# Row maxima and the scores' second product in bfloat16, a ScalarE copy of the products with v, and a new plan of times

## Chip, core and metric

The kernel runs on one core of one Trainium2 chip, as one launch. The metric is device time in microseconds (us), the median of three runs. Engines are named as in the profile: PE is TensorE (matmuls; PEld its weight loads), DVE is VectorE, ACT is ScalarE, POOL is GpSimd, SP is SyncE, which here only issues DMAs.

## What is computed

Attention over queries that are averaged in pairs, then four experts that are mixed per token, then a gated block. Only the attention is touched by the change.

```python
# q, k, v: (2, 8, 1152, 64) float32: 16 heads; q and k drawn wide (about 0.62 standard deviation)
q_pool = q.reshape(B, H, S // 2, 2, D).mean(axis=3)          # 576 queries for each head
scores = scale * np.matmul(q_pool, k.transpose(0, 1, 3, 2))  # 576 x 1152
scores = scores - np.max(scores, axis=-1, keepdims=True)
attn = np.exp(scores)
attn = attn / (np.sum(attn, axis=-1, keepdims=True) + 1e-09)
x = np.matmul(attn, v)
...
x = _moe_ref(x=x, **moe_kwargs)      # 1152 tokens, 512 wide, 4 experts of 1024
return _moe2_ref(x=x, **moe2_kwargs)
```

## The kernel before

The 16 heads go in 8 pairs (`i` = 0 to 7); `s` = 0 or 1 is the head within a pair. For each head there are 9 blocks of 128 keys (`c`), 5 blocks of queries (`j`) and these steps.

- **Transposes.** PE turns the keys (`kt`, line 275) and the pooled queries (`qt`, 329) into PSUM. Both are then split into a float32r high part (`KAB`, `QH`, by ACT, lines 278 and 341) and a rest (`KL`, `QL`, by DVE, 281 and 332). `QZ` holds the queries of both heads, each with zeros in the other head's partitions (ACT lines 342 and 338, POOL 336). The transposes share three PSUM banks (`ps_w`) with the maxima.
- **Spread.** SP copies the parts into `K1` (high, twice), `Q1` (high over rest), `K2` (rest) and `Q2` (high) by DMA (`plan_spread`, 352).
- **Row maxima.** `mp` (line 390): for each query block, three products of `QZ` with 384 columns of `KAB`; DVE reduces the first two in one instruction and the third in another (393). The maxima are joined (407 to 410), turned by PE (`mr`, 425), split (`mh` by ACT, `ml` by DVE) and placed in the first two rows of `Q2` by four small DMAs, so that the score product subtracts them. They are made for pair `i + 1` while pair `i` has its scores.
- **Scores.** `s` (544): for each key block four products of 288 columns, two with `K1`, then two with `K2`, in one of two PSUM slots (`ps_s`). ACT takes the exponential (`pf`, 554), POOL what bfloat16 left of it (`pl`, 565).
- **Products with v.** `av` (587 and 589): 135 matmuls of 64 or 65 columns for each head, half a pair behind the scores, into one PSUM bank (`ps_a`). `vt` holds v scaled, high part by ACT (519) and rest by DVE (523); `vs` is its scale (454 to 458). At the end `out_of` divides by the sums: three DVE instructions (593, 597, 599), for the second batch a fourth (604). The bank is then free for the next head.

**What sets the order.** Each step is put on one list with a time by `at(t, f)`; the list is sorted by time and recorded. Each engine then runs its instructions in that order and waits on semaphores. A unit of time is an 18th of a pair. The constants at the file's top (`KH`, `LO`, `AVW`, `SPOS`, `MX0`, ...) are these times; they change an order, not a speed.

```python
        t = 18 * i
        plan_scores(i, 0, t)
        plan_scores(i, 1, t + 9)
        plan_av(i, 0, t + 9 + AV0, AVN)
        plan_av(i, 1, t + 18 + AV0, AVN if nx else 2)
...
    for _, _, f, args in sorted(agenda, key=lambda x: x[:2]):
        f(*args)
```

A tile name in a profile or an order is the tile's name with its numbers left out (`s`, `mp`, `av`); with numbers, `s3_0_1` is pair 3, head 0, key block 1, and a last number counts tiles.

Of the kernel before, what the change touches and what calls it, by code (L numbers as in the profile page):

```python
# [27 lines left out]
AV0 = 1.49
AVN = 7.48
AVW = ((0.64, 0.05, 1.06, 0.45, 1.0, 0.14, 0.2, 2.36), (0.8, 1.47, 1.71, 2.49, 0.72, 0.32, 0.55, 1.54))  # L30
VH = 0.8
VL = 2.36
VL0 = -5.71
VR = 4.82
VE = 0.2
# [29 lines left out]
KT = (3.05, 3.5)  # L65
QT = 4.54
MX0 = (7.0, 8.1, 9.35, 12.27, 13.06)
SPOS = ((0, 0.8, 2.1, 3, 4.4, 5, 6.2, 7, 7.9), (0.1, 1, 2.1, 3, 4, 5, 6, 7, 7.65))
# [1283 lines left out]
```

## Time and profile before

| | |
|---|---|
| median of three runs | 812.59 us (812.47 to 813.15) |
| the profiled execution | 812.85 us, of which the span from first to last instruction is 811.1 us |
| PE busy | 794.8 us, 98% of the span |
| DVE, ACT, POOL busy | 593.3, 396.0, 295.7 us |
| attention | about 19 to 252 us of the span |
| experts and gated block | the rest; from 300 us on neither code nor plan differs |

One execution was recorded. Matmuls overlap: one lasts longer in the trace than the time after which the next starts, so a price of PE work is read here from the start of one group to the start of the next. A row's time is from the span's start.

### The profile page before, as it was taken

The numbers are of one execution on the slowest core, as the hardware profiler recorded it, in microseconds if no ns is written. First come the engines' busy times: TensorE is split into PE (matmuls) and PEld (weight loads), VectorE is DVE, ScalarE is ACT, GpSimd is POOL, SyncE is SP. The second block draws the span as 40 slices with busy tenths as digits, with TensorE's granted clock in tenths as the row PEclk, the third lists the DMA queues.
The fourth block names the chain that finished last, engine by engine and source line by source line (L and its number), as shares of the span: only waits on it lengthen the run. The fifth ranks groups of instructions, "written<-read, shape, count | busy, mean of one in ns | idle before, by whom it ended". The sixth has DMA issues, their size and how long they took to land.

```text
span 811.1 us, 15625 instructions
## 1 busy us (share of the span) xinstructions
PE 794.8 (98%) x6301; PEld 522.8 (64%) x6301; DVE 593.3 (73%) x1065; ACT 396.0 (49%) x722; POOL 295.7 (36%) x277
## 2 busy tenths in 40 slices
PE   8799999999999999999999999999999999999998
PEld 6598889888877555555545555555554446655787
DVE  6878877887875666779878999979888877872000
ACT  2555565565484443434435556546554544553111
POOL 5787888798750000001101125203331223442100
PEclk9999999999999999999999999999999999999999
DMA  7967776783720121223313332221466842200011
GB/s 184 218 156 163 185 155 135 170 204 83 170 60 2 53 105 53 78 78 104 105 52 104 104 105 83 100 78 52 108 144 127 168 141 74 85 1 1 15 52 52
DMA packets 85975, 83.27 MB, mean 103 GB/s; under 512 B 49624, under 2 KB 67408, under 8 KB 85904
## 3 DMA queue, kind: packets, MB, share of 16 engines
q1 hardware_dynamic: 85904, 82.29, 39.3%
q8 instruction: 49, 0.80, 0.4%
q14 instruction: 22, 0.18, 0.1%
HBM read 51.92 MB, written 2.36 MB: 67 GB/s over the span
## 4 chain that ended last, share of the span: by engine, by line
PE 86%; DVE 10%; DMA 1%; ACT 1%; issue 1%; SPq 0%; ACTq 0%
PE dn L758 21%; PE up L718 21%; PE gt L1290 12%; PE s L544 8%; PE o L1306 6%; PE wf L1259 5%; PE av L589 5%; PE mp L390 5%; DVE mx L393 3%; PE av L587 2%; DVE vt L523 1%; PE kt L275 1%; DVE vs L457 1%; DVE ql L332 1%; DMA rk<-in_k 1%; DMA rw<-in_moe_w 1%
## 5 line engine op out<-in xcount | busy, mean ns | idle before, releaser
L758 PE MATMUL dn<-w,h 128*128 128x512 f16 x840 | 183.9, 379 | 0.0
L565 POOL TENSOR_TENSOR pl<-pf 128x576 f16<-128x576 f32 x141 | 162.7, 1175 | 48.7 <-ACT pf L554 47.5
L718 PEld LDWEIGHTS <-w 128*128 128x128 f16 x1152 | 111.5, 98 | 76.3 <-DVE w L689 0.8
L758 PEld LDWEIGHTS <-h 128*128 128x128 f16 x840 | 81.4, 98 | 96.5 <-ACT up L724 0.7
L554 ACT ACTIVATE pf<-s 128x576 f32<-128x576 f32 x144 | 92.4, 650 | 64.3 <-PE s L544 63.1
L393 DVE TENSOR_REDUCE mx<-mp 128x1 f32<-128x768 f32 (+1 forms) x144 | 101.9, 751 | 19.3 <-PE mp L390 18.7
L718 PE MATMUL up<-xB,w 128*128 128x320 f16 x768 | 109.9, 299 | 0.5 <-DVE xB L807 0.5
L544 PE MATMUL s<-Q,K 128*128 128x288 f32 x576 | 109.2, 313 | 0.2
L857 POOL TENSOR_TENSOR wo<-wo,cv_a 128x512 f32<-128x512 f32 x20 | 25.8, 1293 | 224.7 <-DVE wo L854 127.1
L724 ACT ACTIVATE up<-up 128x320 f32<-128x320 f32 (+1 forms) x96 | 45.8, 477 | 114.3 <-PE up L718 94.1
L718 PE MATMUL up<-xA,w 128*128 128x512 f16 x384 | 89.1, 379 | 0.3 <-DVE w L689 0.3
L589 PE MATMUL av<-vt,pf 128*128 128x65 f16 x720 | 85.0, 194 | 0.1
L544 PEld LDWEIGHTS s<-Q,K 128*128 128x128 f32 x576 | 82.0, 189 | 2.4 <-issue 0.6
L587 PE MATMUL av<-vt,pf 128*128 128x64 f16 x720 | 83.0, 194 | 0.0
L589 PE MATMUL av<-vt,pl 128*128 128x65 f16 x720 | 82.8, 195 | 0.0
L729 DVE TENSOR_TENSOR h<-up,h 128x320 f16<-128x320 f32 (+1 forms) x94 | 50.2, 551 | 42.7 <-ACT h L725 42.3
L1290 PEld LDWEIGHTS <-mw 128*128 128x128 f16 x576 | 55.9, 98 | 36.9
L589 PEld LDWEIGHTS <-pf 128*128 128x128 bf16 x720 | 66.9, 99 | 7.0 <-issue 1.3
L587 PEld LDWEIGHTS <-pf 128*128 128x128 bf16 x720 | 67.0, 98 | 6.9 <-issue 3.3
L589 PEld LDWEIGHTS <-pl 128*128 128x128 f16 x720 | 67.2, 98 | 3.4 <-issue 1.1
L390 PE MATMUL mp<-kab,QZ 128*128 128x384 f32 x216 | 56.5, 367 | 4.4 <-DVE mx L393 2.1
L772 DVE SCALAR_TENSOR_TENSOR x2B<-dn,sh,x2B 128x512 f32<-128x512 f32 x75 | 52.9, 744 | 4.7 <-PE dn L758 4.0
(184 smaller groups left out, 1171.3 us busy)
## 6 DMA issues: line engine op xcount, KB each, us to landing
rw<-in_moe_w SPq DMA_DIRECT2D x64, 512.0 KB
K<-kab SPq DMA_DIRECT2D x32, 288.0 KB
rk<-in_k SPq DMA_DIRECT2D x16, 288.0 KB
rv<-in_v SPq DMA_DIRECT2D x8, 576.0 KB
Q<-qh SPq DMA_DIRECT2D x32, 144.0 KB
K<-kl SPq DMA_DIRECT2D x16, 288.0 KB
rq<-in_q SPq DMA_DIRECT2D x8, 512.0 KB
rw<-in_moe_w_out SPq DMA_DIRECT2D x8, 512.0 KB
```

Source lines behind the costliest of these rows:

```text
L390: mm(ps[:, n, :PC], QZ[:, o : o + P], KAB[i][:, sl], start=True, stop=True)
L393: nc.vector.tensor_reduce(out=mx[i, s][:, j, g : g + 1], in_=st.pop((j, g))[:, :, :PC], axis=AX.XY, op=ALU.max)
L544: mm(ps[:, n, :HALF], a[s][:, cs], b[s][:, n * HALF : (n + 1) * HALF], start=first, stop=not first,)
L554: nc.scalar.activation(out=two(pft[i, s][:, c, :]), in_=st["s"][:, :, :HALF], func=AF.Exp, scale=SCORE)
L565: nc.gpsimd.tensor_tensor(out=o, in0=f, in1=h, op=ALU.subtract)
L587: mm(t[:, j, 0:D], p, vt[s][:, c, 0:D], start=False, stop=False)
L589: mm(t[:, j, :], p, vt[s][:, c, D:], start=(c == 0 and n == 0), stop=(c == NC - 1 and n == 2))
L718: mm(p, w[:, a, c, fc * P : (fc + 1) * P], x[b][:, c, lo - o : hi - o], start=(c == 0 and a == b), stop=(c == KD - 1 and a == 1),)
L729: nc.vector.tensor_tensor(out=hl[:, fc, lo:hi], in0=st["p"], in1=hh[:, fc, lo:hi], op=ALU.subtract)
L758: mm(p, hid[n][a][:, fc, t * P : (t + 1) * P], w[:, b, fc, :], start=(fc == 0 and a == b), stop=(fc == 1 and a == 1),)
L772: nc.vector.scalar_tensor_tensor(out=acc, in0=st["p"], scalar=share, in1=acc, op0=ALU.mult, op1=ALU.add)
L1290: mm(p, mws[n][:, a, m * KD + c], x[:, b * KD + c, lo - o : hi - o], start=(c == 0 and a == b), stop=(c == KD - 1 and a == 1),)
```

## The change

- `K2`, `Q2`, `QZ`, `KL` and the two parts of the maxima (`mh`, `ml`) become bfloat16; `K1`, `Q1`, `KAB`, `QH`, `QL` stay float32r.
- A bfloat16 copy `KB` of the transposed keys is added (`short`, on ACT, one of three on DVE for pair 0); the maxima are taken of `QZ` with `KB`.
- The bfloat16 product comes first in each score group.
- `Q2` is filled from `QZ` by two DMAs instead of from `QH` by one.
- `leave` copies the finished products with v from PSUM into an SBUF tile `as` on ACT. It is put on the list at `t + span + OUT`, `out_of` at `t + span + OUT + OUT2` with `OUT2 = -0.1`.
- The table of times is new.

```diff
-LO = 2.45
+LO = 4.1
...
-    K2 = [k_p.tile([P, S], F32R, name=f"K2_{s}") for s in range(2)]
+    K2 = [k_p.tile([P, S], BF16, name=f"K2_{s}") for s in range(2)]
...
-    Q2 = [k_p.tile([P, T], F32R, name=f"Q2_{s}") for s in range(2)]
...
-    QZ = k_p.tile([P, 2 * T], F32R, name="QZ")
+    Q2 = [k_p.tile([P, T], BF16, name=f"Q2_{s}") for s in range(2)]
...
+    QZ = k_p.tile([P, 2 * T], BF16, name="QZ")
...
+            KB[i] = kq_p.tile([P, S], BF16, tag="kb", bufs=1, name=f"kb{i}")
+            KL[i] = ha_p.tile([P, S], BF16, tag=f"ha{i % 2}", name=f"kl{i}")
...
+            def short(g=g, rows=rows):
+                nc.scalar.copy(out=rows(KB[i]), in_=st[g][:, :, :PC])
...
+            at(t + KT[g] + KH + KS, short)
...
+        def low_k():
+            nc.sync.dma_start(out=K2[s][64:128], in_=KL[i][r])
+
+        def short_q():
+            o = T + TL if s else 0
+            nc.sync.dma_start(out=Q2[s][64:128, : NB * P], in_=QZ[r, o : o + NB * P])
+            o = T if s else NB * P
+            nc.sync.dma_start(out=Q2[s][64:128, NB * P :], in_=QZ[r, o : o + TL])
...
-                mm(ps[:, n, :PC], QZ[:, o : o + P], KAB[i][:, sl], start=True, stop=True)
+                mm(ps[:, n, :PC], QZ[:, o : o + P], KB[i][:, sl], start=True, stop=True)
...
-                nc.vector.tensor_copy(MT[:, 0, :].bitcast(F32R), mf)
+                mb = tiny.tile([P, NB + 1], BF16, tag="mb", bufs=1, name="mb")
+                nc.vector.tensor_copy(mb, mf)
+                nc.vector.tensor_copy(MT[:, 0, :], mb)
...
-                for a, b, first in ((K1, Q1, True), (K2, Q2, False)):
+                for a, b, first in ((K2, Q2, True), (K1, Q1, False)):
...
+        def leave():
+            if (i, s) < (NPAIR - 1, 1):
+                x = tiny.tile([P, NB + 1, D + 1], F32, tag="as", name=f"as{i}_{s}")
+                nc.scalar.copy(out=x, in_=st["t"])
+                st["t"] = x
...
-        at(t + span + OUT, out_of)
+        at(t + span + OUT, leave)
+        at(t + span + OUT + (OUT2 if (i, s) < (NPAIR - 1, 1) else 0), out_of)
```

Three places show how the rows move. The first is PE at the start of pair 3, from the last product with v of head (2, 0); line 544 of before is line 572 of after, 390 is 416. Before:

```order
L589 MATMUL av2_0_1734<-vt0_119,pl2_0_1408 128x65
L544 MATMUL s3_0_0_1973<-Q1_0_125,K1_0_121 128x288 x2
L544 MATMUL s3_0_0_1973<-Q2_0_127,K2_0_123 128x288 x2
L544 MATMUL s3_0_1_1990<-Q1_0_125,K1_0_121 128x288 x2
L544 MATMUL s3_0_1_1990<-Q2_0_127,K2_0_123 128x288 x2
L390 MATMUL mp3_1_3_0_1996<-kab3_1486,QZ_129 128x384 x2
L390 MATMUL mp3_1_3_1_1999<-kab3_1486,QZ_129 128x384
```

The same place after:

```order
L617 MATMUL av2_0_1762<-vt0_119,pl2_0_1429 128x65
L572 LDWEIGHTS K2_0_123
L572 MATMUL s3_0_0_2003<-Q2_0_127,K2_0_123 128x288
L572 LDWEIGHTS K2_0_123
L572 MATMUL s3_0_0_2003<-Q2_0_127,K2_0_123 128x288
L572 MATMUL s3_0_0_2003<-Q1_0_125,K1_0_121 128x288 x2
L416 LDWEIGHTS QZ_129
L416 MATMUL mp3_1_3_0_2024<-kb3_1496,QZ_129 128x384
L416 LDWEIGHTS QZ_129
L416 MATMUL mp3_1_3_0_2024<-kb3_1496,QZ_129 128x384
L416 LDWEIGHTS QZ_129
L416 MATMUL mp3_1_3_1_2027<-kb3_1496,QZ_129 128x384
```

The last maximum product of the pair stands behind one score group instead of two; a bfloat16 product has a weight load of its own in the list, a float32r one carries it within. The second place is ACT at the same point of the program: `vt0` is the high part of v (519, now 547), `pf3_0` are the exponentials, `kab4` and `kb4` the keys of the next pair. Before:

```order
L554 ACTIVATE pf3_0_1971<-s3_0_0_1973 128x576
L519 ACTIVATE vt0_119<-rv3_1206,vs3_1597 128x9x64
L554 ACTIVATE pf3_0_1971<-s3_0_1_1990 128x576
L554 ACTIVATE pf3_0_1971<-s3_0_2_2017 128x576
L429 CAST mh3_1_2061<-mr3_1_2048 5x128
L278 CAST kab4_2050<-kt4_0_2052 128x768
L554 ACTIVATE pf3_0_1971<-s3_0_3_2042 128x576
L278 CAST kab4_2050<-kt4_1_2074 128x384
L554 ACTIVATE pf3_0_1971<-s3_0_4_2109 128x576
```

After:

```order
L547 ACTIVATE vt0_119<-rv3_1316,vs3_1629 128x9x64
L622 COPY as2_0_2022<-av2_0_1762 128x325
L582 ACTIVATE pf3_0_2001<-s3_0_0_2003 128x576
L582 ACTIVATE pf3_0_2001<-s3_0_1_2032 128x576
L582 ACTIVATE pf3_0_2001<-s3_0_2_2048 128x576
L457 CAST mh3_1_2080<-mr3_1_2066 5x128
L282 CAST kab4_2068<-kt4_0_2071 128x768
L285 CAST kb4_2069<-kt4_0_2071 128x768
L582 ACTIVATE pf3_0_2001<-s3_0_3_2060 128x576
L282 CAST kab4_2068<-kt4_1_2102 128x384
L285 CAST kb4_2069<-kt4_1_2102 128x384
L582 ACTIVATE pf3_0_2001<-s3_0_4_2111 128x576
```

`vt0` and the new copy `as2_0` now stand ahead of the pair's first exponential, and each cast of keys is followed by a second one. The third place is DVE where the products of head (2, 0) are divided, after the change:

```order
L419 TENSOR_REDUCE mx3_1_1839<-mp3_1_2_1_1944 128x1
L627 TENSOR_SCALAR dn2_0_2016<-av2_0_1762,vs2_1056 128x5
L631 RECIPROCAL dn2_0_2016<-dn2_0_2016 128x5
L633 TENSOR_TENSOR x0_117<-av2_0_1762,dn2_0_2016 128x5x64
L419 TENSOR_REDUCE mx3_1_1839<-mp3_1_3_0_2024 128x1
```

The division still reads `av2_0`, the PSUM tile, as before, since `out_of` is recorded ahead of `leave`; no row of any engine has an `as` tile as an input. This holds for all 15 copies.

## Rows read from the trace of the kernel before

**Rows 1.** Windows: stretch, its length, busy us by engine, PE clock, DMA share, GB/s.

```profile
19.00:50.00 31.00, 26.44 (x261) 21.55 (x261) 25.13 (x45) 15.62 (x28) 22.87 (x22) 1.00 0.83 190
50.00:77.50 27.50, 27.29 (x390) 24.34 (x387) 22.24 (x39) 16.03 (x27) 23.23 (x23) 1.00 0.71 164
105.10:132.70 27.60, 27.32 (x392) 24.38 (x389) 22.43 (x39) 16.05 (x27) 23.27 (x23) 1.00 0.74 163
187.90:215.50 27.60, 27.43 (x393) 24.42 (x390) 22.56 (x41) 16.05 (x27) 22.35 (x22) 1.00 0.59 137
215.50:252.00 36.50, 34.95 (x545) 28.82 (x542) 24.83 (x50) 21.92 (x38) 18.26 (x16) 1.00 0.30 71
300.00:811.00 511.00, 506.72 (x2751) 285.74 (x2749) 365.03 (x660) 233.65 (x442) 105.78 (x88) 1.00 0.29 82
```

**Rows 2.** Timeline of PE, pair 3 and before it: start, us, instruction, wait before it.

```profile
102.18 0.76 PE L544 MATMUL s<-Q,K 128*128 128x288 f32 x4
102.78 0.20 PE L589 MATMUL av<-vt,pl 128*128 128x65 f16 x1
...
103.22 0.80 PE L390 MATMUL mp<-kab,QZ 128*128 128x384 f32 x3
103.86 0.20 PE L587 MATMUL av<-vt,pf 128*128 128x64 f16 x1
...
105.12 1.29 PE L544 MATMUL s<-Q,K 128*128 128x288 f32 x8
106.25 0.68 PE L390 MATMUL mp<-kab,QZ 128*128 128x384 f32 x3
...
108.94 0.82 PE L275 MATMUL kt<-ident,rk 128*128 128x128 f32 x6
...
116.04 0.80 PE L390 MATMUL mp<-kab,QZ 128*128 128x384 f32 x3 [0.17 <-DVE ql L332]
...
119.09 0.79 PE L544 MATMUL s<-Q,K 128*128 128x288 f32 x4
119.71 0.68 PE L390 MATMUL mp<-kab,QZ 128*128 128x384 f32 x3
120.23 0.69 PE L544 MATMUL s<-Q,K 128*128 128x288 f32 x4
120.76 0.20 PE L589 MATMUL av<-vt,pf 128*128 128x65 f16 x1
...
132.74 1.30 PE L544 MATMUL s<-Q,K 128*128 128x288 f32 x8
```

**Rows 3.** Timeline of PE among the experts' products, 16-bit operands.

```profile
306.26 2.75 PE L718 MATMUL up<-xA,w 128*128 128x512 f16 x12
308.85 3.42 PE L718 MATMUL up<-xB,w 128*128 128x320 f16 x24
...
312.11 2.11 PE L718 MATMUL up<-xA,w 128*128 128x512 f16 x9
```

**Rows 4.** Groups by line, 0 to 420 us: count | busy, mean ns | idle before.

```profile
L725 ACT CAST h<-up 128x320 f16<-128x320 f32 x32 | 13.6, 426 | 1.0
...
L278 ACT CAST kab<-kt 128x768 fp32r<-128x768 f32 x7 | 5.6, 797 | 2.6 <-DMA Q<-qh 1.8 <-PE kt L275 0.9
```

**Rows 5.** Timeline of ACT within pair 3.

```profile
113.13 0.63 ACT L342 CAST QZ<-qt 64x576 fp32r<-64x576 f32 x1
...
119.29 0.78 ACT L519 ACTIVATE vt<-rv,vs 128x576 f16<-128x576 f32 x1 [0.93 <-PE av L589]
119.98 0.65 ACT L554 ACTIVATE pf<-s 128x576 f32<-128x576 f32 x1
```

**Rows 6.** Timeline of DVE within pair 3.

```profile
116.70 1.42 DVE L393 TENSOR_REDUCE mx<-mp 128x1 f32<-128x768 f32 x2 [0.71 <-PE mp L390]
...
120.19 0.49 DVE L599 TENSOR_TENSOR x<-av,dn 128x320 f32<-128x320 f32 x1
```

**Rows 7.** Line 457: durations of one in ns, min/median/max, first and last start.

```profile
L457 DVE TENSOR_SCALAR vs<-vs x8: 169/1045/1102, 19.2 to 196.8; 128x2 f32<-128x2 f32 x8
```

More of the change, by code (lines that the diff above doesn't have):

```diff
@@ L11 @@
 TURN = 1.03
-TURNS = (1.08, 1.18, 2.08, 2.53)
+TURNS = (1.18, 1.53, 1.63, 3.03)
 TURN0 = (0.05, 0.45, 0.55, 0.65)
-KH = 0.49
-KL_ = 0.62
-QH_ = 1.1
+KH = 0.39
+KL_ = 0.27
+QH_ = 1.2
 QL_ = 0.25
-M0 = 0.4
+M0 = 0.25
 M1 = 0.01
@@ L22 @@
 LASTD = ((4,), (0, 7))
-LOL = 0.85
+LOL = 0.95
+KS = 0.1
+KS0 = 0.01
 EX = 0.79
 EX2 = 0.85
-LO = 2.45
+LO = 4.1
 LOV = 1.15
[L28 to L35, printed above, removed]
+AV0 = 1.54
+AVN = 7.33
+AVW = ((0.4, 0.05, 0.51, 0.58, 1.25, 0.14, 0.4, 2.95), (0.48, 0.19, 1.03, 2.49, 1.4, 0.51, 0.69, 1.54))
+VH = 0.65
+VL = 1.91
+VL0 = -2.26
+VR = 4.02
+VE = 1.85
 V1 = (5.5, 1.4)
@@ L38 @@
 QZ0 = 0.25
-QZ1 = 0.1
-VLZ = 2.55
+QZ1 = 0.0
+VLZ = 2.2
 K0 = 1.2
@@ L44 @@
 LV2 = 15.6
-PQ = 0.52
-PQS = 0.65
+PQ = 2.17
+PQS = -0.75
 SH = -5.85
@@ L64 @@
 LATER = 0
[L65 to L68, printed above, removed]
+KT = (3.05, 4.05)
+QT = 4.99
+MX0 = (7.0, 8.15, 9.5, 11.52, 13.11)
+SPOS = ((0, 1.1, 1.95, 2.8, 4.3, 4.9, 6.5, 7, 7.5), (0.1, 0.6, 1.7, 2.7, 4.1, 4.4, 5.55, 7.0, 7.95))
 AVS = 0.02
-AVP = 2.35
+AVP = 1.7
 MXF = (7.3, 8.3, 10, 11.72, 13.01)
-MX1 = (14.0, 16.2, 17.25, 18.82)
-ME = 0.12
+MX1 = (14.15, 16.15, 17.2, 18.67)
+ME = 0.17
 SW = 130.8
 W1 = 133.8
-WT = ((123.5, 129.6, 130.6, 132.7, 138.5, 133.3, 133.5, 135.6, 135.8), (2, 8.8))
+WT =  ((124.7, 129.6, 130.6, 132.7, 138.5, 133.3, 133.5, 135.6, 135.8), (4.4, 8.95))
 WN = (1, 4, 5, 3, 0)
@@ L85 @@
 DT = (140.8, 144.1)
-OUT = 0.35
+OUT = 0.8
+OUT2 = -0.1
 XB = 148.6
@@ L204, in tile_kernel @@
     rq, rt, rk, rv = {}, {}, {}, {}
-    KAB, KL, QH, QL = {}, {}, {}, {}
+    KAB, KL, KB, QH, QL = {}, {}, {}, {}, {}
     pft, pht, plt = {}, {}, {}
@@ L301, in pe, with short @@
                 nc.tensor.transpose(st[n][:, m * P : (m + 1) * P], rk[0][:, 3 * n + m], ident)
+        def short(n):
+            dst = KB[0][:, n * PC : (n + 1) * PC]
+            if n == 1:
+                nc.vector.tensor_copy(dst, st[n])
+            else:
+                nc.scalar.copy(out=dst, in_=st[n])
         def hi(n):
@@ L317, in plan_k_now @@
             at(t + 0.1 * n, pe, n)
+            at(t + 0.1 * n + KS0, short, n)
             at(t + 0.1 * n + 0.05, hi, n)
@@ L362, in plan_spread @@
             cp(Q1[s][64:128], lambda: QL)
-            cp(K2[s][64:128], lambda: KL)
-        cp(Q2[s][64:128], lambda: QH)
+            at(t, low_k)
+        at(t, short_q)
     mx = {}
@@ L427, in cut_hi @@
         def cut_hi():
-            m = st["h"] = tiny.tile([NB + 1, P], F32R, tag="mh", bufs=1, name=f"mh{i}_{s}")
+            m = st["h"] = tiny.tile([NB + 1, P], BF16, tag="mh", bufs=1, name=f"mh{i}_{s}")
             nc.scalar.copy(out=m, in_=st["r"][: NB + 1, 0, :P])
         def cut_lo():
-            m = st["l"] = tiny.tile([NB + 1, P], F32, tag="ml", bufs=1, name=f"ml{i}_{s}")
-            nc.vector.tensor_tensor(out=m, in0=st["r"][: NB + 1, 0, :P], in1=f32(st["h"]), op=ALU.subtract)
+            m = st["l"] = tiny.tile([NB + 1, P], BF16, tag="ml", bufs=1, name=f"ml{i}_{s}")
+            nc.vector.tensor_tensor(out=m, in0=st["r"][: NB + 1, 0, :P], in1=st["h"], op=ALU.subtract)
         def place():
-            for n, m in enumerate((f32(st["h"]), st["l"])):
-                dst = f32(Q2[s][n : n + 1])
+            for n, m in enumerate((st["h"], st["l"])):
+                dst = Q2[s][n : n + 1]
                 nc.sync.dma_start(out=dst[:, : NB * P], in_=m[:NB])
@@ L866, in tile_kernel @@
         for s in range(2):
-            nc.gpsimd.memset(f32(Q2[s][0:64]), 0.0)
-            nc.gpsimd.memset(f32(K2[s][0:64]), 0.0)
-            nc.gpsimd.memset(f32(K2[s][0:3]), -1.0)
-            nc.gpsimd.memset(f32(Q2[s][0:3]), -SHIFT)
+            nc.gpsimd.memset(Q2[s][0:64], 0.0)
+            nc.gpsimd.memset(K2[s][0:64], 0.0)
+            nc.gpsimd.memset(K2[s][0:3], -1.0)
+            nc.gpsimd.memset(Q2[s][0:3], -SHIFT)
             nc.gpsimd.memset(vt[s][:, :, 128:129], 1.0)
@@ L873, in tile_kernel @@
         nc.vector.memset(QP[TL:P, NB], 0.0)
[L874 to L875 removed]
+        nc.vector.memset(QZ[64:128, :T], 0.0)
+        nc.vector.memset(QZ[0:64, T:], 0.0)
         nc.vector.memset(ones, 1.0)
```

8 lines of the change are left out of this document (3 added, 5 removed).

## The prediction

> **What bounds the kernel now.** I read the windows by stage first, then PE's timeline of one pair, then what PE waits for there.
>
> Of the 811.1 us, 511 stand behind 300 us with PE busy 506.7 [rows 1]: nothing there is touched. The attention has three parts. The first pair (19 to 50) takes 31.0 us with PE busy 26.4: its first half is a chain of maxima, not PE work. Six pairs follow, 27.6 us each (105.12 to 132.74 in [rows 2]; the first and the last of the six windows look like the middle one) with PE busy 27.3, POOL 23.3, DVE 22.4, ACT 16.0 [rows 1]. The last pair (215.5 to 252) has no maxima left and PE busy 34.95 of 36.5. So PE sets the pace from 50 to 252 us; behind it POOL has 4.3 us to spare in a pair, DVE 5.2, ACT 11.5. A saving on PE of more than that meets the next engine.
>
> **The change, part by part.**
>
> *Score groups.* Four float32r products behind a product with v take 102.78 - 102.18 = 0.60 us [rows 2]. Two groups in a row take 106.25 - 105.12 = 1.13, so the second costs 0.53: 0.132 for each product, and about 0.08 for entering float32r from 16-bit work, whose loads are too short to cover a float32r load. For 16-bit products: 12 of 512 columns in 308.85 - 306.26 = 2.59 us, 0.216 each; 24 of 320 in 312.11 - 308.85 = 3.26, 0.136 each [rows 3]; that is 0.00042 us a column, so 288 columns cost 0.1225 and 384 cost 0.1625 (estimates from these rows). A new group enters with a bfloat16 product, which needs no long load, and costs 2 x 0.1225 + 2 x 0.132 = 0.51. I take this since a float32r load is already hidden behind a product of 288 columns in the 0.53 group; if the entry price merely moves to the third product it is 0.59. Of 18 groups in a pair some 16 cost 0.60 now: 16 x 0.09 + 2 x 0.02 = 1.5 us saved in a pair (0.2 if the entry price stays).
>
> The Trainium skill (TensorE: Matmul & The Clock Gate, section LDWEIGHTS) puts a load at its columns over 1.2 in ns, 107 for 128. By that the load for `K1` fits under the second bfloat16 product, the group is 0.51, and the 0.59 falls away. No row here has a float32r load behind a 16-bit product of 288 columns, so I keep both ends.
>
> *Maxima.* Three products take 0.52 to 0.53 behind scores (119.71 to 120.23), 0.64 behind products with v (103.22 to 103.86) [rows 2], and 3 x 0.1625 = 0.49 in bfloat16. With six groups of the first kind and three of the second that is 6 x 0.04 + 3 x 0.15 = 0.7 us in a pair. PE's work falls by some 2.2 us.
>
> *ScalarE.* Two casts for `KB` repeat those of `KAB`: 0.80 [rows 4] and, for half the columns, about 0.48. Two copies of 325 columns out of PSUM cost about 0.43 each (the 320-column cast of [rows 4], 0.426). That is 2.1 us more in a pair, 18.2 in all, which fits. But ACT takes things in order. The order shows the copy right behind `vt` and ahead of the first exponential. In the trace `vt` starts at 119.29 and that exponential at 119.98 [rows 5], so it would now start near 120.35 and end near 121.0. PE, after 0.51 + 0.49 + 0.51 + 0.06 from 119.09, wants that exponential's slot at 120.66 for the third score group: a wait of about 0.4 us, and the same at the other head. Nothing reads the copy: DVE divides out of PSUM as before, its last step ending at 120.68 [rows 6] against PE's next product with v at 120.76 [rows 2]. So the bank comes free no sooner, and DVE saves nothing. This part is a loss of 0 to 0.8 us a pair, which the sums below hold.
>
> *SP and DMA.* `K2` and `Q2` halve: 64 x 1152 x 2 bytes instead of 4, and so on. Two more issues in a pair lie on SP, which is not on the path. The DMA share of 0.59 to 0.74 [rows 1] falls.
>
> *DVE.* Its work stays at 22.4 us in a pair while PE asks for it faster. So I walk one pair, 27.62 us, in three stretches.
> - A, from the first scores to `kt` (105.12 to 108.94): 3.82 us. The new order has four score groups, one maxima group, 10 products with v instead of 25 (0.44 us for 14 of them, 102.78 to 103.22) and a short transposition: 2.04 + 0.49 + 0.31 + 0.1 = 2.95, with the wait of 0.4 behind the copy 3.35.
> - B, from `kt` to the first maxima of the next pair (108.94 to 116.04): 7.10 us. The four score groups save 0.4, eight more products with v cost 0.25. The end hangs on DVE: `mp` waited for `ql` [rows 2], and `ql` stands behind line 457, which takes 0.17 or 1.05 us [rows 7]. The new order puts `qt` later and leaves 2.9 us of PE work between it and `mp`, where there were 4.2; so `ql` will be late by 0 to 0.9. B becomes 6.7 to 7.65, I take 7.15: no gain.
> - C, from there to the next pair's first scores (116.04 to 132.74): 16.70 us. PE's work in the new order is 14.4. DVE needs 8 double reductions of 1.42 [rows 6], a division of 0.97 (119.71 to 120.68), `vt`'s rest and small ones, some 14.3 to 15.2 after a first wait of 0.55: it now ends last. C becomes 14.8 to 15.7, I take 15.2.
>
> Together 25.7 (24.8 to 26.8): 1.9 us a pair saved (0.8 to 2.8), six times 11.4 (5 to 17).
>
> On line 457: its two values go with whether POOL is inside an instruction. The Trainium skill (GPSIMD Engine Reference, section Specifications) says that GpSimd shares its SBUF interfaces with VectorE and contends with instructions in a 2-port mode or with two SBUF inputs. By that, POOL busy 23.3 of 25.7 instead of 27.6 makes the 1.05 likelier, B 7.65 and a pair 26.2, or some 3 us more in all. The trace agrees as to the two values; I leave B in the middle.
>
> *Ends.* First pair: its second half gains like the others, about 1.0, the chain of maxima about 0.5: 1.5 (0.5 to 2.5). Last pair: 18 score groups x 0.09 less a little cover that is lost: 1.2 (0.5 to 1.8). Ahead of the scores, `KB` for pair 0 and the extra cast `mb` cost 0.4 (0 to 0.8).
>
> The sum against the profiled execution: 812.85 - 11.4 - 1.5 - 1.2 + 0.4 = 799.2. That execution lies 0.3 above the median of 812.59, so I forecast **799.0**.
>
> **Rivals.**
> - *Half the gain.* The entry price moves to the third product (0.59), and the waits behind the copies stay. For: no row shows that load hidden. Against: loads of this kind hide behind equal columns now. A pair saves 0.2 + 0.7 and little else, 6 x 0.9 + 1.0 + 0.4 - 0.4 = 6.4: about 806.
> - *PE alone decides.* DVE keeps up because its 5.2 us of idle time in a pair were waits for PE. Then PE's own waits, some 1.5 us a pair (the work adds up to 26.1), shrink too and a pair takes 24.6: 6 x 3.0 + 2 + 1.5 = 21.5: about 791 to 794. Against: line 393 and what stands between fill stretch C.
> - *No change.* DVE's chain in B and C doesn't shrink at all and the copies cost 0.8 a pair; only A and the ends gain: within 1.6 us of before.
> - *Slower.* One mechanism: `Q2` of the second head is now read out of `QZ`, as the last of the transfers that start with the pair, and ACT's casts write the same columns for the next pair some 8.0 us later (113.13 - 105.12 [rows 5, 2]). By the tiles' sizes 1105 KB go ahead; at 163 GB/s [rows 1] 6.8 us, at 137 still 8.1. If they land later, ACT stands in the cast, the exponentials behind it wait, both score slots stay full and PE stops: one us a pair for each us of lateness. It decides once they land 10 us after the pair's start, below 110 GB/s; at 11 us a pair loses 1 net, about 819. Against: the bytes shrink by a sixth.
>
> **How the numbers follow.** The forecast, 796 to 802.5: 0.58. Half the gain, 803 to 808: 0.15. PE alone, 790 to 795: 0.12. No change: 0.06. Slower: 0.09. Between 793 and 807.5 lie the forecast, nearly all of the second and half of the third, about 0.8. A measurement of this kernel tells differences above some 0.2%, 1.6 us, from none: faster 0.85, same 0.06, slower 0.09.
>
> **What would show it.** Right: pairs of 25.2 to 26.2 us between 50 and 215 us; a score group of 0.51 and a maxima group of 0.49 on PE's timeline; DVE idle under 3.5 us a pair; waits of PE's third score group for ACT near 0.4 at each head. The first rival shows as 0.59 groups, the second as pairs under 24.9 with DVE above 0.9 busy, the slower one as ACT's `QZ` casts waiting for a DMA. The forecast is wrong if the stretch behind 252 us moves by more than 1 us, or if the pairs differ from each other by more than that.

## The result and the profile after

| | before | after |
|---|---|---|
| median | 812.76 us (812.47 to 813.15) | 818.38 us (817.91 to 819.76) |
| ratio after to before | | 1.0068, 95% interval 1.0056 to 1.008 |
| profiled execution | 812.85 us, span 811.1 | 817.91 us, span 816.1 |
| PE busy | 794.8 us | 781.2 us |
| pair 0; mean of pairs 1 to 6; pair 7 to its last score group | 30.99; 27.59; 28.50 | 29.91; 27.64; 32.35 |

The change is slower by 0.7%, where 799.0 was forecast. PE was busy 13.6 us less, about what the forecast had counted on, and the time rose by 5.6: every saved microsecond, and more, became a wait. The middle pairs are no shorter in the mean (pairs 2 to 4 take 27.17 us, pair 1 takes 29.04), and the last is 3.9 us longer. In `pool_order` and `vt_moved` below, one execution each ran far longer at a much lower granted clock (0.85 and 0.65), and their medians leave it out.

The windows of after (columns as in [rows 1]): the first pair, the two halves of pair 3 (scores of head 0, then of head 1), the last pair, and the stretch that the change does not touch.

```profile
19.30:49.20 29.90, 24.45 (x261) 17.69 (x260) 25.61 (x45) 16.63 (x29) 22.13 (x23) 1.00 0.79 180
105.43:119.24 13.81, 12.82 (x201) 10.84 (x198) 10.09 (x20) 10.60 (x19) 10.24 (x11) 1.00 0.79 173
119.24:132.60 13.36, 12.58 (x196) 10.07 (x192) 11.78 (x20) 7.11 (x12) 12.82 (x13) 1.00 0.51 124
215.05:252.00 36.95, 31.52 (x424) 24.07 (x421) 25.28 (x49) 23.33 (x41) 19.99 (x17) 0.95 0.25 64
305.00:816.00 511.00, 506.23 (x2747) 285.30 (x2745) 363.61 (x658) 232.49 (x442) 105.69 (x88) 1.00 0.30 82
```

The same two halves of pair 3 before, which [rows 1] had only as one row:

```profile
105.12:119.08 13.96, 13.79 (x202) 12.29 (x199) 10.72 (x20) 9.44 (x16) 12.35 (x14) 1.00 0.89 188
119.08:132.73 13.65, 13.54 (x196) 12.09 (x193) 11.72 (x20) 6.61 (x11) 10.94 (x10) 1.00 0.59 137
```

PE lost about one microsecond of work in each half. The first half became 0.15 us shorter, the second 0.29. In the second PE was busy 13.54 of 13.65 us before and is 12.58 of 13.36 after. DVE is busy 11.72 us there before and 11.78 after: its idle time was 1.93 us and is 1.58. The 5.2 us in a pair that the prediction saw as room lay mostly in the first half (3.24).

PE's timeline of after in pair 3 (columns as in [rows 2]):

```profile
105.38 0.68 PE L572 MATMUL s<-Q,K 128*128 128x288 bf16 x4
105.90 0.66 PE L416 MATMUL mp<-kb,QZ 128*128 128x384 bf16 x3
106.40 0.67 PE L572 MATMUL s<-Q,K 128*128 128x288 bf16 x4
...
107.63 0.67 PE L572 MATMUL s<-Q,K 128*128 128x288 bf16 x4 [0.27 <-ACT pf L582]
...
115.07 0.67 PE L572 MATMUL s<-Q,K 128*128 128x288 bf16 x4
...
116.46 0.65 PE L416 MATMUL mp<-kb,QZ 128*128 128x384 bf16 x3 [0.72 <-DVE ql L349]
...
121.34 0.19 PE L617 MATMUL av<-vt,pf 128*128 128x65 f16 x1 [0.45 <-ACT as L622]
...
121.89 0.28 PE L572 MATMUL s<-Q,K 128*128 128x288 bf16 x1 [0.33 <-ACT pf L582]
```

Here are the prices and the new waits together. A score group takes 105.90 - 105.38 = 0.52 us and a maxima group 0.50, both as priced. But PE waits 0.72 for `ql`, and a product with v waits 0.45 for the copy, which nothing reads. The list of waits in the same pair (engine, line, what it waited for: us, times, longest) names the links behind them:

```profile
DVE kl L288 <- ACT kb L285: 1.6, 1, 1.6
...
ACT as L622 <- DVE x L633: 0.9, 2, 0.7
...
PE mp L416 <- DVE ql L349: 0.7, 1, 0.7
DVE ql L349 <- ACT QZ L359: 0.7, 1, 0.7
...
PE s L572 <- ACT pf L582: 0.6, 2, 0.3
PE av L617 <- ACT as L622: 0.5, 1, 0.5
```

`kl` does not read `kb`, `ql` does not read `QZ`, the copy does not read `x` and the products with v do not read the copy. Each of these is an order among instructions on different engines that use one PSUM tile: who is recorded later waits for who is recorded earlier.

The last pair, PE's rows with waits and then POOL:

```profile
220.97 0.16 PE L531 MATMUL cxs<-cxd,ones 128*128 128x2 bf16 x1 [1.44 <-DVE cxd L525]
223.16 0.24 PE L617 MATMUL av<-vt,pl 128*128 128x65 f16 x1 [1.92 <-POOL pl L593]
```

```profile
204.38 8.29 POOL L593 TENSOR_TENSOR pl<-pf 128x576 f16<-128x576 f32 x7 [0.78 <-ACT pf L582]
217.53 7.18 POOL L593 TENSOR_TENSOR pl<-pf 128x576 f16<-128x576 f32 x6 [4.86 <-ACT pf L582]
```

In the new order POOL makes seven rests of head (6, 1), then stands 4.86 us for the first exponential of pair 7, and the last two of (6, 1), for which PE's products stand, come only behind rests of pair 7 by the table of times. From 220 to 225 us the granted clock was 0.81, from 225 to 230 it was 0.85, behind PE's waits of 1.44 and 1.92: a part of each stretch ran at the lower level, 1.2 instead of 2.4 GHz.

### The profile page after: what moved, and what is told of

Same layout as the page of the kernel before. It is cut to its first block, busy times and chain, and to the rows that moved or that the text cites. A ratio compares the mean times of both kernels' runs of the same rounds, so it can differ in the third digit from the quotient of the medians.

```text
span 816.1 us, 15699 instructions
## 1 busy us (share of the span) xinstructions
PE 781.2 (96%) x6301; PEld 496.0 (61%) x6301; DVE 593.6 (73%) x1067; ACT 409.3 (50%) x753; POOL 294.4 (36%) x277
## 4 chain that ended last, share of the span: by engine, by line
PE 78%; DVE 6%; ACT 6%; POOL 3%; DMA 3%; issue 2%; SPq 2%; POOLq 0%; ACTq 0%
PE dn L793 21%; PE up L753 20%; PE gt L1325 11%; PE o L1341 6%; PE wf L1294 5%; PE s L572 5%; PE av L617 4%; PE mp L416 3%; POOL pl L593 3%; PE av L615 2%; DVE mx L419 2%; ACT pf L582 2%; DMA rw<-in_moe_w 1%; DMA rk<-in_k 1%; DVE x L633 1%
## 5 line engine op out<-in xcount | busy, mean ns | idle before, releaser
L593 POOL TENSOR_TENSOR pl<-pf 128x576 f16<-128x576 f32 x141 | 165.1, 1197 | 24.8 <-ACT pf L582 24.1
L572 PE MATMUL s<-Q,K 128*128 128x288 bf16 (+1 forms) x576 | 97.3, 315 | 4.8 <-ACT pf L582 4.7
L416 PE MATMUL mp<-kb,QZ 128*128 128x384 bf16 x216 | 50.8, 325 | 8.5 <-DVE ql L349 4.2
L1325 PE MATMUL gt<-x2Bt,mw 128*128 128x320 f16 x384 | 53.5, 299 | 0.0
```

The lines of the kernel that those rows point to most:

```text
L416: mm(ps[:, n, :PC], QZ[:, o : o + P], KB[i][:, sl], start=True, stop=True)
L572: mm(ps[:, n, :HALF], a[s][:, cs], b[s][:, n * HALF : (n + 1) * HALF], start=first, stop=not first,)
L593: nc.gpsimd.tensor_tensor(out=o, in0=f, in1=h, op=ALU.subtract)
L1325: mm(p, mws[n][:, a, m * KD + c], x[:, b * KD + c, lo - o : hi - o], start=(c == 0 and a == b), stop=(c == KD - 1 and a == 1),)
```

## The experiments

Each run is compared with before in runs on the same chip; before had medians from 813.25 to 813.74 there. "Pairs" are scores to scores in the profiled execution.

### One part undone

**`no_copy`**, after without the copy.

```diff
-        at(t + span + OUT, leave)
```

> The changed kernel without the ScalarE copy of the products with v, which nothing reads. Copy theory (the copy waits for the division on VectorE, so the exponentials behind it and the PSUM bank wait too: in the trace of after PE's third score group, the first products with v, and the same at the other head lose 0.2 + 0.4 + 0.6 + 0.5 us in a pair): pairs fall from 27.2 to 25.5-26.2 us, the whole from 818.4 to 807-811. Rival (the waits behind the copy are replaced by others, ql or POOL, and the copy costs little): pairs at 26.9-27.2, the whole at 816-818.

Measured: 812.36 us, ratio 0.9982 (0.997 to 0.9993). Pairs 2 to 4 take 26.34 instead of 27.17. Both lie outside both expectations, nearer to the theory's. By the ratios, 0.9982 against 1.0068, the copy costs about seven us in all.

**`pool_order`**, after with the last two rests of head (6, 1) ahead of pair 7's.

```diff
-            at(u + (LOV if on_dve else LO if i < NPAIR - 1 else LOL), lo)
+            u_lo = u + (LOV if on_dve else LO if i < NPAIR - 1 else LOL)
+            if i < NPAIR - 1:
+                u_lo = min(u_lo, 18 * (NPAIR - 1) + LOL)
+            at(u_lo, lo)
```

> The changed kernel with one time bounded: POOL's last two remainders of head (6, 1) are recorded ahead of the first one of head (7, 0), as in the kernel before; the copies stay. Order theory (POOL waits 4.9 us for the first exponential of pair 7 while two finished exponentials of pair 6 lie behind in its queue, PE waits 4.5 us for them and its clock falls): the last pair loses 3.9 of its excess, the whole falls to 812.5-814.5. Rival (the last pair is late for the experts' weights, which are loaded later in the new plan): less than 1 us, 817-818.4.

Measured: 813.78, ratio 1.0004 (0.9993 to 1.0015); the last pair 28.74 instead of 32.35, as the order theory had it.

**`kb_after`**, the second cast of keys recorded behind the rest `kl`.

```diff
-            at(t + KT[g] + KH + KS, short)
             at(t + KT[g] + KH + KL_, lo)
+            at(t + KT[g] + KH + KL_, short)
```

> The changed kernel with the bfloat16 cast of the keys recorded behind the rest (kl) instead of ahead of it; all else the same. Theory (readers of one PSUM tile are put in sequence by the build, so kl waits 1.6 us for a cast that it does not need, and ql and the first maxima of a pair are late by 0.9): pairs fall by 0.3-0.8, the whole by 2-5 us to 813-816. Rival (ql is late because of ScalarE's casts of QZ ahead of it, which stay): pairs within 0.2, the whole at 817-819.

Measured: 828.37, ratio 1.0176 (1.0145 to 1.0207), pairs 2 to 4 28.5. The expectation failed: the order of readers was only turned round. Now ACT's cast waits for DVE, and the `QZ` casts and `ql` behind it come later still.

**`no_copy_pool_order`**, the first two together.

> Both of the first two edits. If the two losses are apart from each other, the gains add up: 818.4 - 9 - 5 = about 803 to 806, faster than the kernel before (812.6). If the copy costs little: 812-814.

Measured: 808.35, ratio 0.9936 (0.9917 to 0.9956). Against after that is 1.3% less, where the two edits alone give 0.9 and 0.6: within the intervals the gains add. The expected 803 to 806 was missed, since the copy had been priced at 9 us there. The single times ran from 806.7 to 813.0; in the profiled execution pair 1 took 31.1, the next three 26.3.

### Types or table

**`new_types_old_plan`**: after's code with before's constants (KS, KS0 kept), no copy. **`old_types_new_plan`**: before's code with after's constants.

> The code of after with the table of times of before, and without the copy: what the new types give by themselves. Theory (PE's work fell by 2.2 us a pair as priced; the new table has nothing to do with it): pairs near 26.3 us as in the run without the copy, last pair near 27.5, total 802 to 808. Rival 1 (the new table is needed, since the old one puts the faster products where DVE isn't ready): pairs 27 or more, total 811 or more. Rival 2 (the 1.1 us by which pairs 4 to 6 are longer than pairs 1 to 3 without the copy comes from the types): the same 1.1 us difference here; if it comes from the table, pairs 1 to 6 are alike.

Measured: 809.8, ratio 0.9949 (0.9934 to 0.9964); pairs 2 to 4 26.95, the last 27.56. That lies between the theory and its first rival. Pairs 1 to 5 are alike to 0.2 us.

> The code of before with the table of times of after: the fourth corner of types by table (before 813; new types with the old table 809.8; new types with the new table and without the copy 812.4). Theory (types and table add): PE's float32r work is back, 2.2 us a pair, pairs 27.9 to 28.6; the last pair has POOL's late rests and costs 3 to 5 us more; total 820 to 827. Rival (the new table is the better one for either types, and what it loses it loses in the last pair alone): pairs 27.0 to 27.6, total 812 to 818.

Measured: 823.81, ratio 1.0117 (1.0097 to 1.0137); pairs 28.46, as the theory had it. So the types gain 0.5% with the old table; the new table loses with either types, 812.4 against 809.8 and 823.8 against 813.6.

### The copy: its place or its own time

**`copy_read`**: after with the copy recorded ahead of the division, which then reads it.

```diff
-OUT2 = -0.1
+OUT2 = 0.1
```

> After, with OUT2 = 0.1 instead of -0.1: the division is recorded behind the copy and reads the copy out of SBUF, so the copy no longer waits for DVE and PE's next product with v waits for the copy alone. Theory (the cost of the copy is the chain division, then copy, then product): the copy starts 0.9 us earlier, the stalls of 0.55 us at the next products with v and 0.68 us at the third score group go, a pair falls from 27.17 to about 26.3 and the total to 810 to 813. Rival (the copy's own 0.43 us ahead of the first exponentials is the cost): pairs stay at 26.9 to 27.2 and the total at 816 to 819. In the last pair nothing changes by either (about 32 us).

Measured: 832.85, ratio 1.0218 (1.0179 to 1.0256), pairs 28.41, pair 1 35.0. Both theories missed, and by far. The lines of the division by source show a part of it (duration in ns: least/median/most), first of `copy_read`, then of after:

```profile
L627 DVE TENSOR_SCALAR dn<-as,vs x15: 230/233/4703, 50.1 to 265.9; 128x5 f32<-128x5 f32 x15
...
L633 DVE TENSOR_TENSOR x<-as,dn x15: 424/493/1169, 55.1 to 266.4; 128x320 f32<-128x320 f32 x8, 128x256 f32<-128x256 f32 x7
```

```profile
L627 DVE TENSOR_SCALAR dn<-av,vs x16: 214/224/225, 49.4 to 255.8; 128x5 f32<-128x5 f32 x16
...
L633 DVE TENSOR_TENSOR x<-av,dn x16: 424/458/492, 49.9 to 256.3; 128x320 f32<-128x320 f32 x8, 128x256 f32<-128x256 f32 x8
```

Out of PSUM an instruction on 5 elements takes 0.214 to 0.225 us every time. Out of SBUF it took 4.70 once, while POOL ran six instructions without a gap, and the product 1.16 to 1.17 instead of 0.49 in the second halves of pairs 1 to 4. Besides, DVE now waits for the copy, which the expectation had not counted (list of waits of a pair):

```profile
DVE dn L627 <- ACT as L622: 1.3, 1, 1.3
```

**`copy_of_v`**: after with the copy reading v in SBUF instead.

```diff
-                nc.scalar.copy(out=x, in_=st["t"])
-                st["t"] = x
+                src = rv[min(i + 1, NPAIR - 1)].rearrange("p s c -> p (s c)")[:, : (NB + 1) * (D + 1)]
+                nc.scalar.copy(out=x, in_=src.rearrange("p (j d) -> p j d", d=D + 1))
```

> After, with the copy's source changed: it reads 325 columns of v in SBUF (the tile that the instruction ahead of it on ACT has just read) instead of the products in PSUM; same engine, place, size and output tile, but it is no reader of the PSUM tile. As in after nothing reads the copy. Theory (the copy costs by its place among the readers, behind the division and ahead of the next product): pairs fall from 27.17 to 26.4 to 26.8, total to 811 to 814. Rival (it costs by its own 0.43 us ahead of the exponentials): pairs stay at 27.0 to 27.2, total 816 to 819.

Measured: 816.01 (811.6 to 818.4), ratio 1.0026 (0.9999 to 1.0053). Pairs 2 to 4 take 26.26, below the expected 26.4 and as short as without any copy: its 0.43 us cost nothing, its place among the readers did. The total was outside the range, since pair 1 took 30.05.

### DVE against POOL

**`no_copy_pool_qp`**: `no_copy_pool_order` with POOL's pooling of queries where before had it.

```diff
-PQ = 2.17
-PQS = -0.75
+PQ = 0.52
+PQS = 0.65
```

> No copy, POOL's late rests ahead of the last pair's first ones, and the pooled queries (QP, on POOL) put back to the places of the kernel before. Theory (in pair 1 the rest of v on DVE, two inputs in SBUF, meets a row of POOL's instructions without a gap, and loses up to 5 us to them): with QP's short instructions next to it, it takes 0.8 to 1.8 us in every run, pair 1 is 26.3 to 27 us instead of 31.1, total 803 to 805 and a spread under 2 us instead of 6. Rival (pair 1 is long for another reason): pair 1 stays at 29 or more, total 808.

Measured: 808.66, ratio 0.9936 (0.9921 to 0.9951). Pair 1 took 30.05: the place did not help, v's rest there took 3.95 us.

**`one_input`**: `no_copy_pool_order`, v's rest without its second SBUF input: the subtraction of the high part is left out.

```diff
-        nc.vector.scalar_tensor_tensor(
-            out=vt[s][:, :, 0:64], in0=src, scalar=vs[i][:, s : s + 1], in1=vt[s][:, :, 64:128],
-            op0=ALU.mult, op1=ALU.subtract,
+        nc.vector.tensor_scalar(
+            out=vt[s][:, :, 0:64], in0=src, scalar1=vs[i][:, s : s + 1], scalar2=None, op0=ALU.mult
         )
```

> No copy and POOL's order mended, with the rest of v made by an instruction of one SBUF input (v times its scale; the subtraction of the high part is left out, so the outputs differ). Theory (DVE loses time to POOL only with two inputs in SBUF): the instruction takes 0.6 to 0.8 us each of 16 times, where it was 0.80 to 5.05; pair 1 falls to 26.3 or less, the others by 0 to 0.7 us, total 801 to 805. Rival (any DVE instruction on SBUF data waits for POOL here): durations still 1.0 to 5 us and the total near 808.

Measured: 802.31, ratio 0.986 (0.9845 to 0.9874), pairs 25.87. The line of that instruction in after, and in this run:

```profile
L551 DVE SCALAR_TENSOR_TENSOR vt<-rv,vs,vt x16: 1048/1360/3931, 35.1 to 237.3; 128x576 f16<-128x576 f32 x16
```

```profile
L551 DVE TENSOR_SCALAR vt<-rv,vs x16: 793/803/814, 35.0 to 222.4; 128x576 f16<-128x576 f32 x16
```

With one SBUF input this instruction takes 0.80 us, whatever POOL does.

**`from_high`**: `no_copy_pool_order` with `KB` and `QZ` cast from `KAB` and `QH` in SBUF, so that `kl` and `ql` have no cast of ACT among the readers of their PSUM tile but the one they need. **`from_high_one_input`**: with `one_input` too.

```diff
-                nc.scalar.copy(out=rows(KB[i]), in_=st[g][:, :, :PC])
+                nc.scalar.copy(out=rows(KB[i]), in_=f32(rows(KAB[i])))
...
-                nc.scalar.copy(out=QZ[64:128, to : to + hi - lo], in_=st[0][64:128, lo:hi])
+                nc.scalar.copy(out=QZ[64:128, to : to + hi - lo], in_=f32(QH[i][64:128, lo:hi]))
...
-        at(tv + 0.02, lambda: nc.scalar.copy(out=QZ[0:64, :T], in_=st[0][0:64, :T]))
+        at(tv + 0.02, lambda: nc.scalar.copy(out=QZ[0:64, :T], in_=f32(QH[i][0:64, :T])))
```

> No copy, POOL's order mended, and the second casts of the keys (KB) and ACT's casts of the queries (QZ) read the float32r high part in SBUF instead of the transposed tile in PSUM, so that the rests kl and ql on DVE are no longer ordered behind them as readers of one PSUM tile; ACT does the same casts in the same order. Theory (PE's stall of 0.70 us at the first maxima of the next pair, and DVE's 0.8 and 0.5 us ahead of kl and ql, are this order): pairs fall from 26.34 to 25.5 to 25.8 us, total from 808.4 to 802 to 805. Rival (DVE only waits elsewhere, for PE's next maxima): pairs 26.1 to 26.4, total 807 to 809.

Measured: 808.83, ratio 0.9939 (0.9918 to 0.996), pairs 26.39: the rival's numbers, no gain.

> The same, and the rest of v made by an instruction of one SBUF input (the subtraction is left out, so the outputs differ): all three suspected costs in the pairs are out, the copy, the order of readers, and DVE's loss to POOL. Theory (these three are what the forecast missed in pairs 1 to 6): pairs of 25.0 to 25.6 us, which is the forecast's 25.7 with its wait of 0.4 for the copy taken out, and total 795 to 800. Rival (a fourth cost is open): pairs stay at the 25.87 of the run with one input alone, total 801 to 803.

Measured: 798.73, ratio 0.9818 (0.9804 to 0.9833), pairs 25.38: the forecast's 799.0.

### The instruction whole, in another place

**`vt_moved`**: `no_copy_pool_order` with v's rest for head 0 later, into POOL's idle 3.3 us. **`vt_moved_from_high`** adds the casts of `from_high`; **`vt_moved_from_high_copy`** has the copy back besides.

```diff
-                at(t + 9 * s + (VL if i + s else VL1) + (VLZ if i == NPAIR - 1 and not s else 0), v_lo, i, s)
+                at(t + (9 + VL if s else (4.8 if i < NPAIR - 1 else VL + VLZ) if i else VL1), v_lo, i, s)
```

> No copy, POOL's order mended, and the rest of v for head 0 of pairs 1 to 6 put 2.9 units later on DVE, behind the rests of the keys and into the 3.3 us in which POOL stands still in each pair; the instruction and its results stay whole. Theory (what it loses, it loses to POOL's running instructions): it takes 0.80 to 0.82 us in each of these pairs, also in pair 1 where it took 3.9 to 5.05; pair 1 falls from 30 to 31 us to 26.0 to 26.6, the others to 25.8 to 26.3; total 802 to 805 and a spread under 2 us. Rival (it is long for its place on DVE, or pair 1 has another cause): pair 1 stays above 28, total 807 to 810.

Measured: 806.5, ratio 0.9909 (0.9889 to 0.9928), above the expected 802 to 805. Pair 1 fell to 26.4 as expected, pairs 2 to 4 stayed at 26.3.

> The same with KB and QZ cast from the float32r high parts in SBUF. Theory (the order of readers costs 0.5 us a pair, as between the two runs with one input, and was hidden by the loss to POOL in the run without that): pairs of 25.4 to 25.9, total 799 to 802, below both kernels. Rival (it was no cost at all): as the run before it within 1 us.

Measured: 805.0, ratio 0.9892 (0.9876 to 0.9909), pairs 26.4: not shorter, against the theory.

> The same with the copy put back as in after (recorded behind the division). Theory (the copy is a reader between the division and the next product, and what it costs doesn't hang on the other two causes): 0.8 to 1.0 us more in each of pairs 1 to 6, total 5 to 7 us above the run before it. Rival (it only showed together with the loss to POOL): within 2 us of it.

Measured: 810.07, ratio 0.9959 (0.9944 to 0.9974), pairs 26.89: the copy costs 5 us by itself, 0.49 in each of pairs 2 to 4, which is less than expected, and 1.2 in the last pair.

What held the pairs at 26.3 shows once halves are taken apart. With the new table and types and head 1's rest in its first place, the second half, mean of pairs 2 to 4, stands against that rest's duration like this (six of the fourteen such runs; the others fit as well, but for `copy_read`, whose division loses to POOL too):

| run | second half | v's rest, head 1 | difference |
|---|---|---|---|
| `one_input` | 12.54 | 0.80 | 11.74 |
| `no_copy_pool_order` | 12.77 | 1.03 | 11.74 |
| `vt_moved` | 13.01 | 1.26 | 11.75 |
| after | 13.36 | 1.61 | 11.75 |
| `from_high` | 13.42 | 1.68 | 11.74 |
| `vt_moved_from_high` | 13.55 | 1.80 | 11.75 |

`from_high` and `vt_moved_from_high` did shorten the first half, from 13.56 to 12.97 and from 13.32 to 12.84; by that POOL and DVE met at another moment in the second half, and what the first half won the second lost. Three runs on top of `vt_moved_from_high` put head 1's rest elsewhere to see which number sets the other: **`vt1_mid`** two maxima later, **`vt1_gap`** ahead of `ml`, **`vt1_late`** behind `ml`.

```diff
-                at(t + (9 + VL if s else ...
+                at(t + ((14.9 if i < NPAIR - 1 else 9 + VL) if s else ...
```

(13.3 for `vt1_mid`, 16.3 for `vt1_late`.)

> The same, two maxima later than in vt_moved_from_high, between maxima for which DVE has no idle time. Theory: the half is 11.75 us plus the duration, whatever that comes to. Rival: 13.4 to 13.6 whatever the duration.

Measured: 803.03, ratio 0.9874 (0.9857 to 0.989). The rest took 1.38, the half 13.12: 11.74 and the duration.

> As vt_moved_from_high, with the rest of v for head 1 of pairs 0 to 6 put later on DVE: ahead of the rest of the maxima (ml), where DVE stands still for 0.65 us waiting for ACT. In the runs so far the second half of a pair with the new table is 11.75 us plus the duration of this instruction, to 0.02 us, between 0.80 and 1.81. Theory (DVE's own row of instructions sets the second half, and the gap ahead of ml is the one place where it has room): the half is 11.1 to 11.75 us plus the duration; with a duration of 0.8 to 1.8 the pair is 24.9 to 26.4 and the total 797 to 805. Rival (PE or POOL sets the half, and the duration is long because the half is): the half stays at 13.4 to 13.6 whatever the duration, total 805.

Measured: **800.14**, ratio 0.984 (0.9825 to 0.9855), the fastest with the work whole and 2.2% below after (800.14/818.38). The rest took 1.18, the half 12.70; pairs 25.55.

> The same, one place later, behind ml, where DVE stands still for 0.3 us waiting for PE. Theory: the half is 11.4 to 11.75 us plus the duration; pair 25.2 to 26.4, total 798 to 805. Rival: 13.4 to 13.6 whatever the duration.

Measured: 838.01, ratio 1.0298 (1.0282 to 1.0313). The rest took 6.40, the half 19.3 to 19.7: about 13.2 and the duration, above the theory's sum (by what, is open) but far from the rival's 13.4 to 13.6. DVE's timeline of `vt1_late`, and POOL's at the same time:

```profile
103.40 0.28 DVE L461 TENSOR_TENSOR ml<-mr,mh 5x128 bf16<-5x128 f32 x1 [0.69 <-ACT mh L457]
103.60 6.41 DVE L551 SCALAR_TENSOR_TENSOR vt<-rv,vs,vt 128x576 f16<-128x576 f32 x1
109.93 1.41 DVE L419 TENSOR_REDUCE mx<-mp 128x1 f32<-128x768 f32 x2
```

```profile
103.15 0.46 POOL L252 TENSOR_TENSOR QP<-rq 64x128 f32<-64x128 f32 x1
103.57 1.15 POOL L593 TENSOR_TENSOR pl<-pf 128x576 f16<-128x576 f32 x1
104.67 0.73 POOL L249 TENSOR_TENSOR QP<-rq 128x256 f32<-128x256 f32 x1
105.36 1.14 POOL L593 TENSOR_TENSOR pl<-pf 128x576 f16<-128x576 f32 x1
106.47 0.72 POOL L249 TENSOR_TENSOR QP<-rq 128x256 f32<-128x256 f32 x1
107.15 2.25 POOL L593 TENSOR_TENSOR pl<-pf 128x576 f16<-128x576 f32 x2
```

Six instructions of POOL go ahead of one of DVE that came 0.03 us after the first of them had begun. It ends 0.62 us after the last of them (107.15 + 2.25 = 109.40), when POOL has nothing to do.

## Why the prediction was wrong, point by point

**Right: what PE's work costs.** The score group is 0.51 to 0.52 (predicted 0.51); the first rival's 0.59 is out. Of the nine maxima groups of pair 3 six take 0.48 to 0.50 (predicted 0.49) and three 0.57 to 0.63, which is open. By the Trainium skill (TensorE: Matmul & The Clock Gate, section LDWEIGHTS) a load takes its columns over 1.2 in ns; the 107 ns that this makes for 128 columns, an estimate, fit under a bfloat16 product of 0.1225 us. The price of the group agrees; the loads themselves do not, since the trace gives the float32r ones 189 ns, before and after. The stretch from 305 us on is alike (PE busy 506.2 of 511 us, 506.7 before [rows 1]). No `QZ` cast of ACT stands in the list of waits for a DMA, so the slower rival's mechanism did not come. The kernel was slower by others.

**Right: DVE ends last in stretch C.** The table above and the three runs behind it show it for the second half. In `from_high_one_input` the stretches are 3.1, 7.0 and 15.3 us, where 3.35, 7.15 and 15.2 were predicted. In after they are 3.59 (105.38 to 108.97), 7.49 (to 116.46) and 16.11 (to the next scores at 132.57). Each misses by a term of its own.

**Wrong, C: DVE's waits, put at nothing behind the first.** The prediction took one wait of 0.55 us and 14.3 to 15.2 of work. DVE's timeline of after in that stretch:

```profile
116.98 2.96 DVE L419 TENSOR_REDUCE mx<-mp 128x1 f32<-128x768 f32 x4 [0.67 <-PE mp L416]
...
122.07 1.61 DVE L551 SCALAR_TENSOR_TENSOR vt<-rv,vs,vt 128x576 f16<-128x576 f32 x1
...
128.83 0.28 DVE L461 TENSOR_TENSOR ml<-mr,mh 5x128 bf16<-5x128 f32 x1 [0.70 <-ACT mh L457]
129.42 1.42 DVE L419 TENSOR_REDUCE mx<-mp 128x1 f32<-128x768 f32 x2 [0.31 <-PE mp L416]
131.20 1.42 DVE L419 TENSOR_REDUCE mx<-mp 128x1 f32<-128x768 f32 x2 [0.36 <-PE mp L416]
```

The work was not too small in the sum. Beside the reductions and the division it leaves 2.0 to 2.9 us for "`vt`'s rest and small ones", and they take 1.61 + 0.45; in all DVE is busy 13.9 us there, since its rows overlap a little. But it stands idle 2.2 us, and only 0.52 of that is the first wait. The other 1.7 us, 0.70 of them for ACT's `mh` and most of the others for PE's maxima, had no term, though before had such waits too. So C is 16.11 and not 15.2, and DVE stands idle 5.3 us in the whole pair, where under 3.5 was to show the forecast right.

What could be taken out of C is another matter, and the runs show two things. v's rest takes 1.61 us where 0.80 is its time alone, and with 0.80 C is 15.28 (`one_input`). Put into the wait for `mh`, whole, it leaves C at 15.45 (`vt1_gap`). That 15.28 stands so near to the predicted 15.2 is luck: it is 13.1 us of work and 2.2 of waits.

Before, PE filled the second half, busy 13.54 of 13.65 us. The change took 0.96 us of that away, but the half fell by 0.29 only, since there DVE's chain ends it. The prediction read DVE's room from the pair's row in [rows 1] as 5.2 us and saw it spent in C, but not that the chain in C held waits that stay, and an instruction of which half was waiting for POOL. It did cite the Trainium skill on this (GPSIMD Engine Reference, section Specifications), and used it for line 457 alone. The rule covers every DVE instruction with two SBUF inputs, and v's rest is the largest here. Line 457 itself (485 in after) took 0.17 us in seven of eight places and 0.96 in one, in the first pair: the 1.05 us did not come.

**Wrong, B: `ql`.** 7.49 instead of 7.15, within the bounds (6.7 to 7.65) but for another reason: `kb` and the `QZ` casts stand ahead of `kl` and `ql` among the readers of one PSUM tile (1.6 and 0.7 us in the list of waits). With those casts from SBUF the first half is 0.48 us shorter (13.32 to 12.84 in both comparisons above with head 0's rest at 0.80).

**Wrong, A and the copy.** "Nothing reads the copy ... the bank comes free no sooner" was right, but no sooner was taken for no later. The copy reads the bank too, so it waits for the division and the next product waits for it. Priced at 0 to 0.8 us a pair, taken as 0.4; measured 0.49 in pairs 2 to 4 with the other causes out, and 0.83 in after, where it also shifted v's rest of head 1 from 1.03 to 1.61. The predicted wait of the third score group near 0.4 came where it was expected, as 0.27 and 0.33; PE's wait of 0.45 for the copy, ahead of a product with v, was not in the sum. By the Trainium skill (PSUM — Partial Sum Buffer, section PSUM bank collisions raise a hardware error) two engines may not be at one bank and quadrant at once, reads included, so such readers have to be put in an order. The waits of this trace agree; in after no two readers of one such tile overlap.

**Wrong: the last pair.** Predicted 1.2 us shorter, it is 3.9 longer. The diff showed `LO` from 2.45 to 4.1 beside `LOL` of 0.95; that the difference carries POOL's last two rests behind the next pair's was not worked out. `pool_order` gives 3.6 of it back. The time behind the last score group grew by 1.7 us (568.8 against 567.1), which the prediction had named as a sign of being wrong. It does not go with POOL's order (569.2 in `pool_order`). It is 567.1 in `new_types_old_plan`, but 567.1 and 567.3 also in `no_copy_pool_qp` and `from_high_one_input`, which have the new table but for POOL's pooling of queries in the first; its cause is open.

**Wrong: pair 1.** 29.04 instead of 25.7, 1.9 above the pairs behind it: v's rest of head 0 took 3.93 us there, 0.81 before; in `vt_moved`, with 0.81 again, pair 1 is 26.4. That pairs differ by more than 1 us was another such sign.

**The sum.** The span missed by 18.8 us: 11.7 in pairs 1 to 6, 5.0 in the last, 1.7 behind it, 0.4 in the first. In a pair such as pair 3 it is 0.48 (order of readers), 0.49 (copy) and 0.81 (v's rest) above the 25.39 of `from_high_one_input`, which makes 27.17, as measured. Pairs 5 and 6 take 0.5 us more than these in after, and 0.2 to 2.2 more in most other runs with the new types and table. Their second half is 12.21 instead of 11.74 us and the duration of v's rest in after, `no_copy` and `one_input`. That goes with the fourth instruction of the division in the second batch; it was not tried apart.

## What to carry to other kernels

Take DVE's idle time from the half of the loop where it is the last, not from the whole loop, ask which of its waits there are links of its own chain, and look at each of its instructions with two SBUF inputs for the time that it has without POOL. An added read of a PSUM tile by another engine is a link in a chain: look who is recorded ahead of it and behind it, even if nothing uses what it reads. When a table of times is made anew, compare the order on the engine with the fewest waits too; two rests in the wrong place cost here 4 to 5 us, as much as the new types gave with the old table.

## What the runs showed of the hardware

- A DVE instruction with two SBUF inputs that comes while POOL runs one ends about 0.61 us after that one: 1.18, 1.38 and 1.61 us for 0.57, 0.77 and 1.00 us left of it. POOL's next instruction then takes 1.66 us instead of 1.15. By the Trainium skill (SBUF — State Buffer, section Who interferes with whom) whoever starts first holds the shared ports for its whole instruction; the trace agrees so far.
- It goes further than that section says. When DVE came 0.01 to 0.07 us ahead of POOL's next instruction, that one passed too (1.77 to 1.83 us). When it came 0.01 to 0.04 us behind the start of one, three to six passed, 3.93 to 6.41 us in ten cases, each ending about 0.62 us after POOL's unbroken row did. Two cases of the kind (6.03 us in `vt1_late`, 4.70 in `copy_read`) had come in the middle of one; why is open. `vt1_gap` and `vt1_late` differ by one place of one instruction and by 38 us.
- With one input in PSUM (the division of after) or one in SBUF (`one_input`) the same engine lost nothing beside the same POOL instructions. One tensor input in SBUF is not always safe, though: line 457 has one and took 1.05 us beside POOL [rows 7], and the first instruction of the division in `copy_read` has one and took the 4.70.
